# Issuing the first products of two blocks together in the even steps of chunk 0 of a pooled-attention and squared-ReLU kernel

## The chip, the cores and the metric

The kernel runs on one core of one Trainium2 chip. The metric is device time in microseconds (us) of one execution; less is better. The times shown are those of three runs of the same kernel, and one more execution was taken with the hardware profiler; the rows below come from that one.

## The reference

Inputs are q, k and v (8 batches, 8 heads, 576 tokens, 64 channels per head) and two weight matrices, `w_in` (512 x 2048) and `w_out` (2048 x 512), in float32.

```python
k_p = k.reshape(B, H, Sp, pool, D).mean(axis=3)        # pool = 8, Sp = 72
v_p = v.reshape(B, H, Sp, pool, D).mean(axis=3)
scores = scale * np.matmul(q, k_p.transpose(0, 1, 3, 2))
attn = np.exp(scores - np.max(scores, axis=-1, keepdims=True))
attn = attn / (np.sum(attn, axis=-1, keepdims=True) + 1e-09)
x = np.matmul(attn, v_p)          # heads side by side: 4608 tokens x 512
h = np.maximum(x @ w_in, 0.0)     # "first product"
out = h * h @ w_out               # "second product"
```

## The kernel before, in words

The 4608 tokens are worked on in 12 chunks of 384 tokens (`CH`, `NCH`). For each chunk the attention part makes x, kept transposed (channels on partitions, tokens along the free axis). The feed-forward part then goes through the 2048 hidden channels in 16 blocks of 128 (`NFC`). One pair (chunk, block) is a **step**; steps are numbered s = 16 x chunk + block, so steps 0 to 15 are chunk 0.

In a step, `hidden` (line 502) issues the first product of block s on TensorE (PE) into a PSUM bank, tile `h`, from the pool `ps_h`, which has two banks (line 100). From block 6 of chunk 0 on (`SPLIT = 6`) each float32 operand is split into a high and a low part (tiles `xh`, `xl` and `w_i`), and the first product is 12 matmuls: 4 pieces of 128 channels, three products each. The first six of the 12 read the weight tile `w_i_0`, the other six `w_i_2`; blocks 6 and 7 read the same two tiles, as do 8 and 9, and so on. `project` (line 539) issues the second product of block s - 2 (`LAG = 2`) into the output banks `o`. In chunk 0 it is 3 plain float32 products (6 rows in the trace), which read the block's activations `r` and the weight tile `wf_o`.

The function that `hidden` returns, `activate`, is called at the end of the step: ScalarE (ACT) reads the bank `h`, writes its ReLU to `r`, and squares it. Only that read of `h` makes the bank free for the block after the next.

Between `hidden` and `project` stand the PE parts of the attention for later chunks, which `on_pe` names: turning q (`qps`), scores (`sps`), turning the exponents (`pps`, `token_turn`) and weighing the values (`av`). Their PSUM tiles share three banks (`ps_a`). After the PE rows of a step come its rows on the other engines, in the order of the loop at the end of the program: reading those banks, the softmax, and the preparation of weights. In chunk 0 the weights still come in as 64-bit words, and each is turned to float32 and split: `magnitude` on ACT, `to_float32` on VectorE (DVE), and a cast on ACT with a subtraction on DVE in `split_weights`. The weights for chunk 0 are made just ahead of the blocks that read them, so in these steps ACT and DVE are as loaded as PE.

Every engine works through its own rows in program order (`InOrder`, line 23). The attention of chunk 1 has, for each pair of heads p, five stages in five steps from step 3p on: turn q; scores (`token_scores`) with the row maxima `tm` on DVE and the exponents `te` on ACT; `token_normalise` on DVE; `token_turn`; `weigh_values`. Pair 3's scores lie in step 10, its normalising in step 11, its turn in step 12 and its values in step 13. From step 10 the attention of chunk 2 begins: q of pair 0 is turned in step 10 and split into `st` (ACT, then DVE), and read by the scores in step 11; q of pair 1 in step 14, scores in step 15.

Of the kernel before, what the change touches and what calls it, by code (L numbers as in the profile page):

```python
# [37 lines left out]
def pooled_attn_relu2_ffn(  # L38
# [25 lines left out]
    NFC = DFF // P  # L64
# [19 lines left out]
    SPLIT = 6  # L84
# [37 lines left out]
    def issue_loads():  # L122
        for dst, src in loads:
            dma(dst, src)
        loads.clear()
# [39 lines left out]
    def to_float32(*keys):  # L165
        parts = []
        for key in keys:
            words, m = raw.pop(key).rearrange("p a (n w) -> p a n w", w=2), wf[key].rearrange("p (a n) -> p a n", a=2)
            parts.append((words, m, m.bitcast(U32)))
        for _, m, _ in parts:  # L170
            DVE.tensor_scalar(m, m, EXP_MIN, EXP_MAX, op0=ALU.max, op1=ALU.min)
        for words, _, m in parts:
            DVE.scalar_tensor_tensor(m, m, 3, words[..., 0], op0=ALU.logical_shift_left, op1=ALU.bitwise_or)
        for words, _, m in parts:
            DVE.scalar_tensor_tensor(m, words[..., 1], 0x80000000, m, op0=ALU.bitwise_and, op1=ALU.bitwise_or)
# [326 lines left out]
    def hidden(c, fc):  # L502
        hp = ps_h.tile([P, 512], F32, name=f"h_{c}_{fc}", tag="h")
        cb, o = fc * P // WC, fc * P % WC
        prods = []
        for cc in range(NCC):
            key, cols = ("i", cb, cc // 2 * 2), slice(cc % 2 * WC + o, cc % 2 * WC + o + P)
            if c == 0 and fc < SPLIT:
                prods += [(wf[key][:, cols], x0[cc // 2][:, cc % 2, :])]
            else:  # L510
                prods += [(wt[key][:, w, cols], xts[c][x][:, cc, :]) for w, x in ((0, 0), (0, 1), (1, 0))]
        for i, (w, x) in enumerate(prods):
            PE.matmul(hp[:, :CH], lhsT=w, rhs=x, start=i == 0, stop=i == len(prods) - 1)

        def activate():
            if c == 0:
                r = sb.tile([P, CH], F32, name=f"r_{c}_{fc}", tag="gh", bufs=LAG + 1)
            else:
                r = sb.tile([P, CH], F32, name=f"r_{c}_{fc}", tag="r", bufs=2)
            ACT.activation(r, hp[:, :CH], AF.Relu)  # L520
            if c < 2:
                ACT.activation(r, r, AF.Square)
            else:
                DVE.tensor_tensor(r, r, r, op=ALU.mult)
            gts[c, fc] = r

        return activate

    def split_hidden(c, fc):
        if c == 0:  # L530
            return
        gh = sb.tile([P, CH], F32R, name=f"gh_{c}_{fc}", tag="gh", bufs=LAG + 1)
        gl = sb.tile([P, CH], F32R, name=f"gl_{c}_{fc}", tag="gl", bufs=LAG + 1)
        split(gh, gl, gts[c, fc])
        gts[c, fc] = (gh, gl)
# [3 lines left out]
    def project(c, fc):  # L539
        if fc == 0:  # L540
            accs[c] = [ps_o.tile([P, 512], F32, name=f"o_{c}_{t}", tag=f"o{t}") for t in range(NTT)]
        g, key = gts.pop((c, fc)), ("o", fc)
        for t in range(NTT):
            tt = slice(t * P, (t + 1) * P)
            if c == 0:
                prods = [(g[:, tt], wf[key])]
            else:
                prods = [(g[x][:, tt], wt[key][:, w, :]) for x, w in ((0, 0), (0, 1), (1, 0))]
            for i, (a, w) in enumerate(prods):
                PE.matmul(accs[c][t], lhsT=a, rhs=w, start=fc == 0 and i == 0, stop=fc == NFC - 1 and i == len(prods) - 1)  # L550

        def store():
            for t in range(NTT):
                ob = sb.tile([P, DM], F32, name=f"ob_{c}_{t}", tag="ob", bufs=OB)
                ACT.copy(ob, accs[c][t])
                dma(out[c * CH + t * P:c * CH + (t + 1) * P, :], ob)

        return store if fc == NFC - 1 else None


    steps = [(c, fc) for c in range(NCH) for fc in range(NFC)]
# [105 lines left out]
    for c in range(1, NCH):  # L667
# [6 lines left out]
        for p in range(NPAIR):  # L674
            s = c * NFC + first[p]
# [5 lines left out]

    last = (to_float32, split_weights)
    on_pe = (transpose_k, transpose_q, scores, token_scores, token_turn, weigh_values)
    for s in range(-PRO, len(steps) + LAG):
        todo = work.get(s, [])
        activate = hidden(*steps[s]) if 0 <= s < len(steps) else None
        later = [f(*a) for f, a in sorted(((f, a) for f, a in todo if f in on_pe), key=lambda x: x[0] is weigh_values)]
        store = project(*steps[s - LAG]) if s >= LAG else None
        if 0 <= s - 1 < len(steps):
            split_hidden(*steps[s - 1])  # L690
        for f in later:
            f()
        for f, a in todo:
            if f not in on_pe + last:
                f(*a)
        keys = [a[0] for f, a in todo if f is to_float32]
        if keys:
            to_float32(*keys)
        for f, a in todo:
            if f is split_weights:  # L700
                f(*a)
        issue_loads()
        for f in (activate, store):
            if f:
                f()
# [30 lines left out]
```

## Time and profile before

| | us |
|---|---|
| median of 3 runs | 964.59 |
| lowest and highest | 963.69, 967.23 |
| profiled execution, its own time | 964.33 |
| span in the profile of that execution | 962.6 |

| engine | busy us | share of the span |
|---|---|---|
| PE (matmuls) | 946.1 | 98% |
| DVE | 615.0 | 64% |
| ACT | 451.5 | 47% |
| GpSimd (POOL) | 348.8 | 36% |

Busy shares are means over the whole span. The stretch that the change touches, blocks 6 to 15 of chunk 0, lies between 74.2 and 133.2 us from the start of the span; there PE is busy 56.69 of 59.00 us, DVE 49.79 and ACT 47.48, at a granted PE clock of 1.00. PE's bars overlap, as a matmul is still draining when the next one enters, so that times on PE are best read from start to start.

### The profile page before, as it was taken

How to read it: one execution, taken by the hardware profiler on the slowest of the kernel's cores; microseconds unless marked ns; L12 is line 12 of the kernel's file. 1: busy time of each engine (PE TensorE's matmuls, PEld its weight loads, DVE VectorE, ACT ScalarE, POOL GpSimd, SP SyncE). 2: the span in 40 equal slices, each digit the busy share in tenths (PEclk: the TensorE clock that was granted, in tenths of full speed). 3: DMA queues.
4: the chain of work that ended last, by engine and by line, in shares of the span. 5: the costliest groups of instructions: out<-in, count | busy, mean ns of one | idle time of the engine just before them, and what ended most of it. 6: DMA issues, size and time to landing. Idle time of an engine off the chain costs nothing.

```text
span 962.6 us, 13481 instructions
## 1 busy us (share of the span) xinstructions
PE 946.1 (98%) x4944; PEld 803.6 (83%) x4944; DVE 615.0 (64%) x1028; ACT 451.5 (47%) x909; POOL 348.8 (36%) x215
## 2 busy tenths in 40 slices
PE   7899999999999999999999999999999999999998
PEld 6456668888888888888888888888888888888997
DVE  7889886667865566677765656767776565453221
ACT  3789776754444344444344344434443434532322
POOL 3800144444444434344353444344443534440000
PEclk9799999999999999999999999999999999999999
DMA  9963112113112112112112112112211110100000
GB/s 256 319 237 116 61 33 78 35 50 98 52 31 77 32 34 67 48 52 82 52 44 77 30 35 79 38 30 69 82 50 39 68 32 18 58 10 9 33 1 34
DMA packets 51651, 63.65 MB, mean 66 GB/s; under 512 B 13936, under 2 KB 32192, under 8 KB 51584
## 3 DMA queue, kind: packets, MB, share of 16 engines
q1 hardware_dynamic: 51584, 62.78, 21.2%
q8 instruction: 39, 0.64, 0.3%
q14 instruction: 28, 0.23, 0.1%
HBM read 53.08 MB, written 9.68 MB: 65 GB/s over the span
## 4 chain that ended last, share of the span: by engine, by line
PE 88%; DVE 5%; DMA 4%; ACT 2%; issue 1%; SPq 0%; ACTq 0%; DVEq 0%
PE o L34 41%; PE h L34 39%; PE av L34 3%; PE sps L34 3%; DVE wf_o L34 2%; DVE wf_i L34 1%; PE qps L34 1%; DMA raw_o<-in_moe_w_out_dram 1%; DMA v<-in_v_dram 1%; DMA k<-in_k_dram 1%; ACT te L34 1%; DMA vv<-in_v_dram 1%; DMA raw_i<-in_moe_w_in_dram 1%; DVE tm L34 1%; DVE w_i L34 1%
## 5 line engine op out<-in xcount | busy, mean ns | idle before, releaser
L34 PE MATMUL h<-xh,w_i 128*128 128x384 f32 x1488 | 416.9, 341 | 0.0
L34 PE MATMUL o<-w_o,gh 128*128 128x512 f32 x1056 | 334.8, 398 | 0.0
L34 PEld LDWEIGHTS h<-xh,w_i 128*128 128x128 f32 x1488 | 272.8, 188 | 10.6 <-issue 1.4
L34 POOL PARTITION_ALL_REDUCE tot<-sc x80 | 201.4, 2564 | 210.1 <-issue 199.6
L34 PE MATMUL h<-xl,w_i 128*128 128x384 f32 x744 | 249.9, 336 | 0.0
L34 PEld LDWEIGHTS o<-w_o,gh 128*128 128x128 f32 x1056 | 192.4, 188 | 51.9 <-issue 16.5
L34 POOL PARTITION_ALL_REDUCE mx<-sc x80 | 117.8, 1519 | 287.1 <-ACT sc L34 287.1
L34 DVE TENSOR_TENSOR gl<-r,gh 128x384 fp32r<-128x384 f32 x176 | 143.5, 815 | 109.1 <-ACT gh L34 108.9
L34 PE MATMUL o<-w_o,gl 128*128 128x512 f32 x528 | 209.1, 396 | 0.0
L34 DVE TENSOR_TENSOR r<-r 128x384 f32<-128x384 f32 x160 | 105.6, 660 | 109.1 <-ACT r L34 108.8
L34 ACT CAST gh<-r 128x384 fp32r<-128x384 f32 x176 | 90.4, 514 | 150.3 <-DVE r L34 149.8
L34 PEld LDWEIGHTS h<-xl,w_i 128*128 128x128 f32 x744 | 139.7, 188 | 10.6 <-issue 2.9
L34 ACT ACTIVATE r<-h 128x384 f32<-128x384 f32 x192 | 94.2, 491 | 100.5 <-PE h L34 99.1
L34 PEld LDWEIGHTS o<-w_o,gl 128*128 128x128 f32 x528 | 99.1, 188 | 22.1
L34 DVE TENSOR_TENSOR st<-qps,st 64x384 fp32r<-64x384 f32 x80 | 60.8, 760 | 59.1 <-ACT st L34 58.3
L34 ACT CAST st<-qps 64x384 fp32r<-64x384 f32 x80 | 59.5, 744 | 56.9 <-PE qps L34 56.5
L34 ACT CAST xh<-rb 128x384 fp32r<-128x384 f32 x40 | 20.5, 513 | 94.6 <-DVE rb L34 94.6
L34 ACT ACTIVATE sc<-sc 72x384 f32<-72x384 f32 x80 | 39.7, 525 | 46.4 <-DVE sc L34 46.4
L34 DVE TENSOR_REDUCE vp<-v 72x64 f32<-72x512 f32 x48 | 51.0, 1062 | 0.0
L34 PE MATMUL av<-sc,vp 72*64 72x384 f32 (+1 forms) x256 | 45.6, 436 | 3.6 <-ACT sc L34 2.1
L34 PE MATMUL o<-wf_o,r 128*128 128x512 f32 x96 | 44.4, 598 | 0.0
L34 DVE TENSOR_REDUCE kp<-k 96x64 f32<-96x512 f32 x42 | 43.8, 1043 | 0.2 <-DMA k<-in_k_dram 0.2
(82 smaller groups left out, 702.1 us busy)
## 6 DMA issues: line engine op xcount, KB each, us to landing
k<-in_k_dram SPq DMA_DIRECT2D x48, 192.0 KB
out_dram<-ob SPq DMA_DIRECT2D x36, 256.0 KB
raw_i<-in_moe_w_in_dram SPq DMA_DIRECT2D x16, 512.0 KB
raw_o<-in_moe_w_out_dram SPq DMA_DIRECT2D x16, 512.0 KB
v<-in_v_dram SPq DMA_DIRECT2D x56, 144.0 KB
rb<-rd SPq DMA_DIRECT2D x80, 96.0 KB
q<-in_q_dram SPq DMA_DIRECT2D x30, 192.0 KB
q<-in_q_dram SPq DMA_DIRECT2D x32, 96.0 KB
```

Source lines behind the costliest of these rows:

```text
L34: return lambda *a, **k: self.tc.keep_in_program_order(f(*a, **k))
```

## The change

For s from 6 to 14 in the even steps, `hidden` is called for block s and at once for block s + 1, and in the odd step that follows it isn't called. `activate` of each block stays where it was, at the end of the block's own step.

```diff
     on_pe = (transpose_k, transpose_q, scores, token_scores, token_turn, weigh_values)
+    ahead = {}
     for s in range(-PRO, len(steps) + LAG):
         todo = work.get(s, [])
-        activate = hidden(*steps[s]) if 0 <= s < len(steps) else None
+
+        two = SPLIT <= s < NFC and s % 2 == 0
+        for n in range(s, s + 1 + two):
+            if 0 <= n < len(steps) and n not in ahead:
+                ahead[n] = hidden(*steps[n])
+        activate = ahead.get(s)
```

The order of the rows on DVE, ACT, POOL and SP is the same before and after; only PE's rows move. In the rows below a name ends in a serial number, `h_7` is block 7 of chunk 0, `r_4` the activations of block 4, and `sps_3` pair 3's scores; the first row of each group of like rows stands for the group.

PE in steps 6 and 7, before:

```order
L34 MATMUL pps_1_0_825<-ident,te_1_738 72x96 x4
L34 MATMUL qps_2_835<-ident,q_2_644 128x96 x4
L34 MATMUL o_0_625<-wf_o_633,r_4_771 128x512
L34 MATMUL h_7_871<-xh_685,w_i_0_704 128x384
L34 MATMUL sps_2_0_884<-kf_185,st_2_846 96x72
L34 MATMUL av_1_894<-sc_1_843,vp_184 64x192 x2
L34 MATMUL o_0_625<-wf_o_633,r_5_809 128x512
```

The same place with the change:

```order
L34 MATMUL h_7_825<-xh_685,w_i_0_704 128x384
L34 MATMUL pps_1_0_838<-ident,te_1_738 72x96 x4
L34 MATMUL qps_2_848<-ident,q_2_644 128x96 x4
L34 MATMUL o_0_625<-wf_o_633,r_4_771 128x512
L34 MATMUL sps_2_0_884<-kf_185,st_2_859 96x72
L34 MATMUL av_1_894<-sc_1_856,vp_184 64x192 x2
L34 MATMUL o_0_625<-wf_o_633,r_5_809 128x512
```

Block 7's first product has gone ahead of `pps`, `qps` and the second product of block 4, straight behind block 6's. Steps 8, 12 and 14 are alike.

PE in steps 10 and 11, before:

```order
L34 MATMUL sps_3_0_1047<-kf_185,st_2_846 96x72
L34 MATMUL qps_0_1057<-ident,q_0_855 128x96 x4
L34 MATMUL av_2_1062<-sc_2_1009,vp_184 64x192 x2
L34 MATMUL o_0_625<-wf_o_850,r_8_975 128x512
L34 MATMUL h_11_1111<-xh_685,w_i_0_930 128x384
L34 MATMUL sps_0_0_1124<-st_0_1084,kl_322 72x384
L34 MATMUL o_0_625<-wf_o_850,r_9_1031 128x512
```

The same place with the change:

```order
L34 MATMUL h_11_1047<-xh_685,w_i_0_930 128x384
L34 MATMUL sps_3_0_1060<-kf_185,st_2_859 96x72
L34 MATMUL qps_0_1070<-ident,q_0_868 128x96 x4
L34 MATMUL av_2_1075<-sc_2_1009,vp_184 64x192 x2
L34 MATMUL o_0_625<-wf_o_863,r_8_988 128x512
L34 MATMUL sps_0_0_1124<-st_0_1097,kl_322 72x384
L34 MATMUL o_0_625<-wf_o_863,r_9_1031 128x512
```

Pair 3's scores and the turn of chunk 2's q now stand behind block 11's first product; between that turn (`qps_0`) and the scores that read its result (`sps_0`) there is now no first product.

## Rows read from the trace of the kernel before

**Rows 1.** The page, busy time by engine over the span.

```profile
PE 946.1 (98%) x4944; PEld 803.6 (83%) x4944; DVE 615.0 (64%) x1028; ACT 451.5 (47%) x909; POOL 348.8 (36%) x215
```

**Rows 2.** Waits of PE from 60 us to the end: us, times, longest.

```profile
PE av L34 <- ACT te L34: 1.6, 1, 1.6
PE pps L34 <- DVE te L34: 0.8, 1, 0.8
```

**Rows 3.** Chain that ended last, 60 to 170 us: start, us, what.

```profile
115.11 2.60 PE o L34 x6
117.71 2.09 PE h L34 x12
```

**Rows 4.** Timeline of PE, steps 6 to 8: start, us, row, count.

```profile
76.73 0.82 PE L34 MATMUL pps<-ident,te 96*72 96x96 f32 x8
...
86.41 0.74 PE L34 MATMUL h<-xh,w_i 128*128 128x384 f32 x1
...
88.92 2.74 PE L34 MATMUL o<-wf_o,r 128*128 128x512 f32 x6
```

**Rows 5.** Timeline of ACT, steps 6 to 12; in brackets idle before, and releaser.

```profile
76.56 0.48 ACT L34 ACTIVATE r<-h 128x384 f32<-128x384 f32 x1
...
84.48 1.78 ACT L34 ACTIVATE te<-sps,tm 96x72 f32<-96x72 f32 x8 [1.97 <-DVE tm L34]
...
89.26 0.52 ACT L34 ACTIVATE r<-h 128x384 f32<-128x384 f32 x1
...
98.36 0.54 ACT L34 ACTIVATE r<-h 128x384 f32<-128x384 f32 x1
...
111.68 0.49 ACT L34 ACTIVATE r<-h 128x384 f32<-128x384 f32 x1
```

**Rows 6.** Timeline of PE, steps 2 and 3.

```profile
49.73 2.85 PE L34 MATMUL h<-x,wf_i 128*128 128x384 f32 x8 [1.17 <-ACT r L34]
...
56.20 2.85 PE L34 MATMUL h<-x,wf_i 128*128 128x384 f32 x8 [1.04 <-ACT r L34]
```

**Rows 7.** Timeline of PE, steps 10 to 12.

```profile
99.36 0.90 PE L34 MATMUL sps<-kf,st 64*96 64x72 f32 x16
...
102.29 0.87 PE L34 MATMUL av<-sc,vp 72*64 72x192 f32 x8 [1.56 <-ACT te L34]
...
107.86 0.34 PE L34 MATMUL sps<-st,kl 128*72 128x384 f32 x1
...
110.73 0.74 PE L34 MATMUL h<-xh,w_i 128*128 128x384 f32 x1
...
112.01 0.51 PE L34 MATMUL h<-xh,w_i 128*128 128x384 f32 x2
...
114.14 0.96 PE L34 MATMUL pps<-ident,te 96*72 96x96 f32 x8 [0.76 <-DVE te L34]
```

**Rows 8.** Timeline of DVE, steps 10 and 11.

```profile
100.55 0.46 DVE L34 TENSOR_REDUCE tm<-sps 96x4 f32<-96x288 f32 x1
...
104.68 1.77 DVE L34 TENSOR_TENSOR st<-qps,st 64x384 fp32r<-64x384 f32 x2 [2.91 <-ACT st L34]
...
111.04 1.31 DVE L34 TENSOR_TENSOR w_i<-wf_i,w_i 128x512 fp32r<-128x512 f32 x1
...
113.54 0.82 DVE L34 TENSOR_TENSOR te<-te,tm 96x288 f32<-96x288 f32 x2
```

**Rows 9.** Timeline of PE, steps 14 and 15.

```profile
125.30 0.50 PE L34 MATMUL qps<-ident,q 96*128 96x96 f32 x4
...
130.32 0.34 PE L34 MATMUL sps<-st,kl 128*72 128x384 f32 x1
```

**Rows 10.** Timeline of DVE, step 14.

```profile
127.56 1.72 DVE L34 TENSOR_TENSOR st<-qps,st 64x384 fp32r<-64x384 f32 x2 [1.76 <-ACT st L34]
```

**Rows 11.** Windows of PE: length, busy us (rows), granted clock, DMA share, GB/s.

```profile
30.00:35.00 5.00, 3.38 (x13) 0.79 1.02 333
35.00:40.00 5.00, 4.65 (x17) 0.50 1.04 394
40.00:45.00 5.00, 5.00 (x19) 0.69 1.07 350
45.00:50.00 5.00, 3.83 (x27) 1.00 0.85 262
```

## The prediction

> **What bounds the kernel now.** I read the page first: PE is busy for 98% of the span [rows 1], so the time ends where PE's rows end, and a change of order pays only by the idle time of PE that it removes or adds. The waits of PE come next. From 60 us to the end there are two, 1.6 us for the exponents `te` on ACT and 0.8 us for the normalised `te` on DVE [rows 2]; both lie in the stretch that the change touches. So the most that this change can give back is 2.3 us of 964, or 0.24%. Then the lengths on PE, from the chain of waits: a second product of chunk 0 takes 2.60 us and a first product 2.09 us [rows 3]. Below, H7 is the first product of block 7, P4 the second product of block 4. The timelines of ACT and DVE come last: each `activate` row stands far behind the first product that it reads. H8 begins at 86.41 us [rows 4], while the ReLU of block 7, the block before it, runs from 89.26 to 89.78 us [rows 5]. ACT and DVE lag behind PE by most of a step here, and PE works on because the order before gives it other work in between.
>
> **What the change does.** It adds and removes no instruction, on any engine; DVE, ACT, POOL and SP (with every DMA) keep their order. On PE, H7, H9, H11, H13 and H15 each move ahead of the attention rows and the second product of the even step. That does two things. The moved H needs its PSUM bank one second product and the step's attention rows earlier. And in an even step everything behind the moved H, attention rows and P, comes 2.09 us later, so that whoever reads those attention rows gets them later. The rows of an odd step come at the old time, unless PE was held.
>
> **Costs, one by one,** as lateness of PE against its old times.
>
> *H7.* It now follows H6 directly, where `pps` stood, at 76.73 us [rows 4]. Its bank is free when the ReLU of block 5 ends, at 76.56 + 0.48 = 77.04 us [rows 5]. That PE does wait for such a ReLU is seen in steps 2 and 3, by 1.17 and 1.04 us [rows 6]. Wait: 77.08 - 76.73 = **0.35**. Queued behind it are `pps`, `qps` and P4; ACT gets `pps` 2.09 + 0.35 = 2.44 late.
>
> *H9.* H8 ended at 88.92, where P6 starts [rows 4], so H9 stands ready at 88.92 + 0.35 = 89.27. It needs the ReLU of block 7, which ended at 89.78 [rows 5]. ACT has become 2.44 late in step 6, but had a pause of 1.97 ahead of the exponents at 84.48 [rows 5]; 0.47 is left and the ReLU ends at 90.25. Wait: **1.0**. If ACT absorbs all, it is 0.5; if nothing, 2.95. I take 1.0, since the pause is in the trace. PE is 1.35 late.
>
> *H11, H13, H15* find their bank free. For H11: the ReLU of block 9 ended at 98.90 [rows 5], with 1.35 more 100.25; H11 stands ready where `sps` stood, 99.36 + 1.35 = 100.71 [rows 7]. For H13: the ReLU of block 11 ended at 112.17 [rows 5], with the 3.15 of step 10 below 115.32; H13 comes after 116. A rule of the Trainium skill (Perfetto Trace Analysis, Optimization Strategy) speaks against the change here: it says that a gap which repeats regularly on the engine that should be saturated can mean too few buffers for the next tile. With two banks, five pairs and 0.35 to 1.0 a pair, that would make 1.75 to 5 us; by the rows only two pairs pay, together 1.35, and I go by the rows.
>
> *Step 10, the exponents.* Pair 3's scores start at 99.36 + 1.35 + 2.09 = 102.80 and last 0.90 [rows 7], to 103.70. Before, DVE came to them at 100.55, just 0.3 after they were done [rows 8]: it was DVE that was late. Now DVE waits for PE and is 103.70 - 100.55 = 3.15 late, and with it all that hangs on it. `av`, which waits for a bank that the exponents free, comes at 102.29 + 3.15 = 105.44; so the old wait of 1.56 [rows 7] is hardly shortened.
>
> *Step 11, scores of chunk 2.* They need `st`, which DVE ended at 104.68 + 1.77 = 106.45 [rows 8], now 109.60. H11 covered that before; now only P8 does (105.44 + 0.87 + 2.60 = 108.91). They start at 109.60 and not at 107.86 [rows 7]: PE is 1.74 late.
>
> *H12.* It starts at 110.73 + 1.74 = 112.47 [rows 7]. Its 7th matmul, 1.45 later (112.01 - 110.73 to the 6th [rows 7], and 2.09 / 12 = 0.17 more), reads the second weight tile, which DVE ended at 111.04 + 1.31 = 112.35 [rows 8], just in time; now 115.50. Wait: 115.50 - 113.92 = **1.6**, lateness 3.3. This is the least certain term. DVE's row of 1.31 ran beside a reduction on POOL, which comes later too: from 0 to 1.6, and I take all of it.
>
> *Step 12, the normalised exponents.* They are ready at 113.54 + 0.82 + 3.15 = 117.51 [rows 8]; `pps` now comes at 115.50 + 1.04 + 2.09 = 118.63, so the old wait of 0.76 [rows 7] is gone. Against 114.14 + 2.09, PE is 2.4 late.
>
> *Steps 14 and 15.* `qps` starts at 125.30 + 2.4 + 2.09 = 129.79 [rows 9]. From its start to the end of DVE's `st` took 127.56 + 1.72 - 125.30 = 3.98 [rows 9, 10], and DVE was waiting for ACT, which had just got `qps` [rows 10], so the length stays. The scores can start at 133.77; PE has at most 0.50 + 2.60 to put in between, as H15 has gone ahead. Before, they started at 130.32 [rows 9]. Lateness **3.45**, 1.05 of it new.
>
> Beyond that PE has no wait to give back [rows 2], so it is not regained. **Sum:** 0.35 + 1.0 + 0.4 (step 11) + 1.6 - 0.9 (step 12) + 1.05 = about 3.45 us. Pairing two first products saves nothing itself: 2.09 + 2.60 a step are already matmul after matmul. The profiled execution took 964.33 us, so 964.33 + 3.45 = **967.8 us**; the median of the runs is 0.26 above the profiled time, within their spread. That is 0.35% more, and about 0.5% (4.8 us) is what a measurement here can tell from no change.
>
> **Rivals.**
>
> *The waits only change place* (963 to 965.5). DVE and ACT take up the lateness as they do after step 7, H12 finds its weights, and PE loses 1.35 at the banks and 1.05 in step 15, and wins back up to 2.3 [rows 2]: 964.4. For it: DVE had 2.91 of waiting in step 10 [rows 8]. Against: that waiting hangs on the exponents themselves, which come later.
>
> *Slower by over 0.5%, through ACT* (969.7). The lateness of step 6 isn't absorbed: the cast that DVE needs ahead of pair 2's maxima sits behind the late `pps` rows on ACT, so the pause at 84.48 moves along instead of shrinking [rows 5]. H9 then waits 2.95 instead of 1.0 and all behind it is 1.95 later: 967.8 + 1.95. It decides once the ReLU of block 7 ends after about 91.9 us.
>
> *Slower through the clock* (972.9). From 35 to 40 us PE had a granted clock of 0.50, the 1.2 GHz level, after 3.38 busy of 5 us; the shortfall over 30 to 45 us is 5 x (0.21 + 0.50 + 0.31) = 5.1 us [rows 11]. If the new waits bring that on, 967.8 + 5.1. The Trainium skill (TensorE: Matmul & The Clock Gate, Why this matters for your kernels) warns that idle gaps between bursts of matmuls bring the slow clock back. Against it: waits of 1.17 and 1.04 us [rows 6] passed at a clock of 1.00 in 45 to 50 us [rows 11], and the new ones are mostly of that size, five in 60 us.
>
> *Faster by over 0.5%* would need 4.8 us, and PE has only 2.3 us of waits to lose.
>
> **How the numbers follow.** Forecast 0.63, waits that change place 0.17, ACT 0.11, clock 0.06, something unseen that is faster 0.03. The forecast and the second case lie within 0.5% (0.80); the two slower rivals lie outside (0.17). The range runs from 964.4, the second case's value, to 971.5: the upper bound of the H9 term with 1.8 for a part of a clock loss or a second such wait. It leaves out most of the clock case and the lower half of the second.
>
> **What would show it.** Right: waits of PE for the ReLU at H7 and H9; `tm` of pair 3 starting right after `sps` near 103.7; a wait of `h` for `w_i` at H12; a wait of `sps` for `st` of about 1 us in step 15; no `pps` wait in step 12; clock 1.00. Wrong: no wait at H9, DVE back on its old times by 115 us, PE at block 0 of chunk 1 before 134.5 (it was at 133.2; I expect 136.6), or a clock below 1 there.

## The result and the profile after

| | before | changed |
|---|---|---|
| median of 10 runs, us | 964.86 | 968.10 |
| lowest and highest, us | 963.49, 970.45 | 967.80, 969.27 |
| ratio of the times, 95% interval | | 1.0034 (1.0021 to 1.0047) |
| profiled execution, span, us | 962.6 | 966.1 |
| start of H6, the first product of block 6 | 74.22 | 73.54 |
| start of block 0 of chunk 1 | 133.20 | 136.20 |
| the stretch between the two | 58.98 | 62.66 |

The forecast was 967.8 us, with 3.45 us more in the stretch. The stretch has 3.68 more in the two profiles, and the medians differ by 3.24. That is less than the 0.5% that the prediction took as the least to be told from no change, but the whole interval of the ratio lies above 1, so the changed kernel is slower. The rows that bound the stretch, in the kernel before and then in the changed one:

```profile
74.22 0.74 PE L34 MATMUL h<-xh,w_i 128*128 128x384 f32 x1
...
133.20 0.74 PE L34 MATMUL h<-xh,w_i 128*128 128x384 f32 x1
```

```profile
73.54 0.74 PE L34 MATMUL h<-xh,w_i 128*128 128x384 f32 x1
...
136.20 0.74 PE L34 MATMUL h<-xh,w_i 128*128 128x384 f32 x1
```

Behind the stretch the two profiles hardly differ: 962.6 - 133.20 = 829.4 us and 966.1 - 136.20 = 829.9 us.

As H6 itself starts at a slightly different time in every execution (0.68 us earlier in that of the changed kernel), places are compared below by their distance from H6.

First the waits of PE from 60 us to the end, in the changed kernel (engine, line, releaser: us, times, longest):

```profile
PE av L34 <- ACT te L34: 1.3, 1, 1.3
PE h L34 <- ACT r L34: 1.3, 2, 1.1
PE sps L34 <- ACT w_i L34: 1.0, 1, 1.0
```

Beside [rows 2]: the wait for the exponents `te` has stayed, that of `pps` for the normalised exponents has gone, and two kinds are new, first products that wait for a ReLU, and the scores of step 15. The releaser that the last line names is a cast on ACT that had nothing to do with them; the split of q on DVE is what ended just before, as its row below shows.

PE's timeline in the changed kernel (start, us, row; in brackets idle before and releaser):

```profile
76.39 0.44 PE L34 MATMUL h<-xh,w_i 128*128 128x384 f32 x1 [0.18 <-ACT r L34]
...
78.60 0.82 PE L34 MATMUL pps<-ident,te 96*72 96x96 f32 x8
...
89.93 0.44 PE L34 MATMUL h<-xh,w_i 128*128 128x384 f32 x1 [1.08 <-ACT r L34]
...
92.14 2.74 PE L34 MATMUL o<-wf_o,r 128*128 128x512 f32 x6
...
102.57 0.90 PE L34 MATMUL sps<-kf,st 64*96 64x72 f32 x16
...
105.25 0.87 PE L34 MATMUL av<-sc,vp 72*64 72x192 f32 x8 [1.30 <-ACT te L34]
106.05 4.54 PE L34 MATMUL o<-wf_o,r 128*128 128x512 f32 x6
109.80 0.96 PE L34 MATMUL sps<-st,kl 128*72 128x384 f32 x1
...
115.28 0.61 PE L34 MATMUL h<-xh,w_i 128*128 128x384 f32 x2
...
118.19 0.82 PE L34 MATMUL pps<-ident,te 96*72 96x96 f32 x8
...
133.30 0.37 PE L34 MATMUL sps<-st,kl 128*72 128x384 f32 x1 [1.01 <-ACT w_i L34]
```

These answer to [rows 4, 7, 9]. H7 and H9 wait where the prediction put them (in step 8 there are no attention rows, so H9 passes P6 alone). The row at 106.05 is new in another way: P8's bar is 4.54 us long, where that of P6, the same six rows, has 2.74 in [rows 4].

ACT's timeline, to be read beside [rows 5]:

```profile
75.86 0.48 ACT L34 ACTIVATE r<-h 128x384 f32<-128x384 f32 x1
...
79.13 0.92 ACT L34 COPY sc<-pps 72x384 f32<-72x384 f32 x2 [2.23 <-PE pps L34]
...
84.61 1.77 ACT L34 ACTIVATE te<-sps,tm 96x72 f32<-96x72 f32 x8 [0.43 <-DVE tm L34]
...
89.39 0.49 ACT L34 ACTIVATE r<-h 128x384 f32<-128x384 f32 x1
```

ACT now waits 2.23 us for `pps`, as H7 stands ahead of it, and the old pause of 1.97 us ahead of the exponents has shrunk to 0.43.

DVE's timeline, beside [rows 8, 10]:

```profile
83.25 0.69 DVE L34 TENSOR_TENSOR w_i<-wf_i,w_i 128x512 fp32r<-128x512 f32 x1 [0.73 <-ACT w_i L34]
...
103.50 0.45 DVE L34 TENSOR_REDUCE tm<-sps 96x4 f32<-96x288 f32 x1 [2.48 <-PE sps L34]
...
107.63 1.70 DVE L34 TENSOR_TENSOR st<-qps,st 64x384 fp32r<-64x384 f32 x2 [2.91 <-ACT st L34]
...
113.92 1.31 DVE L34 TENSOR_TENSOR w_i<-wf_i,w_i 128x512 fp32r<-128x512 f32 x1
...
131.45 1.71 DVE L34 TENSOR_TENSOR st<-qps,st 64x384 fp32r<-64x384 f32 x2 [3.82 <-ACT st L34]
```

The maxima of pair 3 now wait 2.48 us for PE, where DVE came to them late before, and the rows behind them follow at their old distances. In the last row `st` ends at 133.16, and the scores of step 15 start at 133.30.

And the granted clock of PE (length, busy, clock, DMA share, GB/s):

```profile
106.00:107.00 1.00, 1.00 (x4) 0.92 0.03 8
107.00:108.00 1.00, 1.00 (x2) 0.50 0.00 0
108.00:109.00 1.00, 1.00 (x3) 0.50 0.00 0
109.00:110.00 1.00, 1.00 (x4) 0.50 0.00 0
110.00:111.00 1.00, 1.00 (x5) 0.87 0.00 0
```

For some 3.4 us PE ran at half speed, the 1.2 GHz level, just behind the wait for the exponents. Summed over these windows that is 0.08 + 3 x 0.50 + 0.13 = 1.7 us of PE's work lost. The prediction had this as a rival that adds 5.1 us to the rest. Did these 1.7 us make the time, in place of the waits that I had predicted?

### The profile page after: what moved, and what is told of

It reads as the page before. It is cut to its first block, busy times and chain, and to the rows that moved or that the text cites. A ratio compares the mean times of both kernels' runs of the same rounds, so it can differ in the third digit from the quotient of the medians.

```text
span 966.1 us, 13480 instructions
## 1 busy us (share of the span) xinstructions
PE 947.9 (98%) x4944; PEld 803.5 (83%) x4944; DVE 614.4 (64%) x1028; ACT 451.4 (47%) x909; POOL 348.9 (36%) x215
## 4 chain that ended last, share of the span: by engine, by line
PE 88%; ACT 4%; DMA 3%; DVE 3%; SPq 1%; issue 1%; DVEq 0%; ACTq 0%
PE o L34 40%; PE h L34 39%; PE av L34 3%; PE sps L34 3%; DMA raw_i<-in_moe_w_in_dram 2%; PE qps L34 1%; DVE wf_o L34 1%; DMA k<-in_k_dram 1%; SPq L34 1%; ACT te L34 1%; DVE wf_i L34 1%; DMA q<-in_q_dram 1%; ACT r L34 0%; ACT wf_o L34 0%; ACT st L34 0%
```

## The experiments

Theory A is the prediction's: the moved first product waits for its bank, and the attention rows behind it reach DVE late, whose chain then sets when block 12 gets its weights. Theory B: the fall of the clock is the cost. Theory C: pairing costs a fixed amount per pair. D and E are named where they are tested. Each kernel was timed beside the kernel before on the same chip, whose median there was 964.15 to 964.44 us; the ratio is that of the two times. "Stretch" is from H6 to block 0 of chunk 1 in the one execution that was profiled, where before has 58.98 us.

### The gap filled, so that the clock holds (fill_wait)

```diff
         qt = loaded.pop(("q", c, p))
+        for i in range(8 if (c, p) == (2, 0) else 0):
+            PE.matmul(pt[:, :P], lhsT=ident, rhs=ident, start=True, stop=True)
```

> The changed kernel with 8 matmuls of the identity put on PE in step 10 ahead of the turn of chunk 2's q, into the bank that the turn then overwrites; 1.1 us of PE work where PE waited 1.3 us for the exponents. Theory A: the clock stays at 1.00 from 106 to 111 us, and the time stays as in the changed kernel (968.1 us, within 0.5), because the second weight tile of block 12 is ready at 115.2 us either way: the freed 1.7 us turns up as a wait of H12 of about 1.5 us. Theory B: the time falls by about 1.7 us to 966.4 us.

Measured: 967.77 us, ratio 1.0043 (1.0028 to 1.0058), stretch 62.77 (H6 at 74.08, block 0 at 136.85). Its windows (as above, with PE, PEld, DVE, ACT and POOL busy ahead of the clock) and its waits:

```profile
104.00:108.00 4.00, 4.00 (x32) 3.12 (x31) 1.14 (x4) 3.19 (x10) 0.00 (x0) 1.00 0.00 2
108.00:112.00 4.00, 3.78 (x12) 1.80 (x11) 3.77 (x7) 3.94 (x10) 0.00 (x0) 1.00 0.00 0
```

```profile
PE h L34 <- ACT r L34: 1.3, 2, 1.1
PE sps L34 <- ACT w_i L34: 1.0, 1, 1.0
PE h L34 <- DVE w_i L34: 0.9, 1, 0.9
PE sps L34 <- DVE st L34: 0.4, 2, 0.2
```

Rows of PE, then the row of DVE that H12 waits for:

```profile
103.95 2.05 PE L34 MATMUL qps<-ident 128*128 128x128 f32 x16
...
106.26 0.87 PE L34 MATMUL av<-sc,vp 72*64 72x192 f32 x8
```

```profile
115.21 0.68 DVE L34 TENSOR_TENSOR w_i<-wf_i,w_i 128x512 fp32r<-128x512 f32 x1
```

The clock stayed at 1.00, and the time didn't move. The 1.7 us came out again in three places. The eight matmuls took 1.89 us (the turn of q follows at 105.84) and not the 1.1 expected, so that `av` starts 0.47 us later than in the changed kernel, by the distance from H6 (106.26 - 74.08 against 105.25 - 73.54). The scores of step 11 wait for `st` (0.2 in the list), and H12 waits for `w_i` (0.9). These two are waits that the prediction had and that the changed kernel's list doesn't show: slow PE filled them there. What ends both kernels' delay is the same tile: DVE's `w_i` ends 41.69 us after H6 in the changed kernel and 41.81 here. Theory B, 966.4 us, falls for the changed kernel.

### The waits for the banks taken away (relu_early)

```diff
         for f in later:
             f()
+        if s in (5, 7):
+            activate()
+            activate = None
         for f, a in todo:
```

> The changed kernel, but in steps 5 and 7 the activation (ReLU and square) stands on ScalarE right behind the attention rows of the step, ahead of the work on the weights. Only ScalarE's order in two steps differs. Theory A: the waits ahead of H7 and H9 (0.2 and 1.1 us) are gone, all that follows on PE, VectorE and ScalarE comes 1.2 to 1.3 us earlier, and the stretch from H6 to block 0 of chunk 1 falls from 62.66 to 61.4 us; 966.8 us. Theory D (what binds from step 10 on is VectorE's own load, and an earlier PE doesn't help): unchanged, 968.1 us.

Measured: 966.11 us, ratio 1.0026 (1.0003 to 1.0049), stretch 60.79 (73.72 to 134.51). Its waits:

```profile
PE av L34 <- ACT te L34: 1.3, 1, 1.3
PE sps L34 <- ACT w_i L34: 1.0, 1, 1.0
PE sps L34 <- DVE st L34: 0.2, 1, 0.2
```

The two waits are gone, and the stretch is 1.87 shorter, more than the 1.26 that the idle column of the changed kernel had shown for them (0.18 + 1.08). By the starts it is 0.50 at H7 (H6 to `pps`: 5.06 us in the changed kernel, 4.56 here) and 1.37 at H9 (H8 to P6, 92.14 - 86.20 = 5.94 and 90.45 - 85.88 = 4.57), together 1.87: all of it reached block 0 of chunk 1. The idle column counts from the end of the last bar, while without a wait the next row starts before that end, and so it leaves out about 0.3 us of each such wait. The interval of the ratio is too wide to tell A from D; the trace does: DVE's `w_i` for block 12 ends 39.83 us after H6 (112.24 + 1.31 - 73.72), 1.86 earlier than in the changed kernel, so an earlier PE does help and theory D falls.

### The second first product behind the attention rows (behind_attention)

```diff
-        for n in range(s, s + 1 + two):
-            if 0 <= n < len(steps) and n not in ahead:
-                ahead[n] = hidden(*steps[n])
+        if 0 <= s < len(steps) and s not in ahead:
+            ahead[s] = hidden(*steps[s])
...
+        rows = [(f, a) for f, a in todo if f in on_pe]
+        later = [f(*a) for f, a in rows if f is not weigh_values]
+        if two:
+            ahead[s + 1] = hidden(*steps[s + 1])
+        later += [f(*a) for f, a in rows if f is weigh_values]
```

> All five pairs, but in an even step the second first product stands behind the attention rows that VectorE and ScalarE wait for (pps, qps, sps) and ahead of the values and the second product. Theory A: no wait at H7, 1.1 us at H9 as step 8 has no attention rows, none for the exponents in step 10 as H11 covers it, none for the split q in step 15, so of the 3.7 us that the stretch from H6 to block 0 of chunk 1 has gained about 1.0 is left (the H9 wait, and VectorE's own path to the weights of block 12 and the normalised exponents of step 12, which is 0.8 late): 60.0 us against 58.98 before and 62.66 changed; 965.3 us. Theory C (the cost lies in pairing itself): 62.7 us and 968.1.

Measured: 965.63 us, ratio 1.0008 (0.9993 to 1.0023), stretch 61.25 (73.76 to 135.01).

```profile
PE h L34 <- DVE w_i L34: 1.0, 1, 1.0
PE pps L34 <- DVE te L34: 0.8, 1, 0.8
PE h L34 <- ACT r L34: 0.8, 1, 0.8
```

All five second first products still stand in the even step (only H9 directly behind its H8), and most of the cost is gone: the interval leaves out theory C's 968.1. The waits at H7, for the exponents and in step 15 are gone; that at H9 is left, and so are the two in step 12 that DVE's chain sets, as expected. Up to `pps` of step 12 the lateness is 0.79 (114.47 - 73.76 against 114.14 - 74.22), near the 1.0 expected; 1.48 more came behind it, where H13 took 3.23 us from start to start at a lower clock (windows as above):

```profile
114.00:115.00 1.00, 0.53 (x4) 0.76 0.00 0
115.00:116.00 1.00, 1.00 (x7) 0.50 0.00 0
116.00:117.00 1.00, 1.00 (x4) 0.50 0.00 0
117.00:118.00 1.00, 1.00 (x5) 0.53 0.00 0
```

Here a slow clock did cost in the profiled execution: no wait of PE comes behind it in the stretch that could hide it.

### One pair at a time (pairs_6_8, pair_10, pair_12, pair_14)

The only edit is the condition:

```diff
-        two = SPLIT <= s < NFC and s % 2 == 0
+        two = s in (6, 8)
```

and `s == 10`, `s == 12`, `s == 14` in the others.

> Only blocks 6+7 and 8+9 are paired. Theory A (the bank of the moved first product is not yet read by ScalarE, and the attention rows behind it reach VectorE late): PE waits for a ReLU ahead of H7 by 0.2 us and ahead of H9 by 1.1 us, block 0 of chunk 1 starts about 1.0 to 1.3 us later than the 133.2 us of before, 965.3 us. Theory B (the low clock after a gap of PE is the cost): no low clock without the pair of step 10, so no more than 0.3 us, 964.7 us. Theory C (each pair costs the same, a fifth of 3.4 us): 1.4 us, 965.8 us.

> Only blocks 10+11 are paired. Theory A: pair 3's maxima start on VectorE near 102.4 instead of 100.55 us, the second weight tile of block 12 is ready 1.9 us later, H12 waits for it, and the old wait of step 12 stays as there is no moved H13: block 0 of chunk 1 1.9 to 2.1 us late, 966.3 us. Theory B: 1.7 us if the clock falls to 0.5 behind the wait of the values, nothing if it doesn't. Theory C: 0.7 us, 965.0 us.

> Only blocks 12+13 are paired. Theory A: H13 covers the wait for the normalised exponents (0.8 us by the wait, 0.9 by the starts) and nothing else changes: the stretch falls from 58.98 to 58.1 us, 963.4 us. Theory C (each pair costs the same): 0.7 us more, 965.0 us.

> Only blocks 14+15 are paired. Theory A: the scores of chunk 2 in step 15 wait 1.05 us for the split q, as the length from the turn to the end of the split is 3.98 us and PE has only 2.9 us of work in between; 965.4 us. Theory B: nothing, 964.4 us. Theory C: 0.7 us, 965.0 us.

> The same kernel as in the run of the pair 14+15 alone, with more rounds, since there the median (968.4) and the stretch from H6 to block 0 of chunk 1 (60.54 us) did not agree. Theory A: the stretch is 60.0 to 60.6 us and the median about 1.2 to 1.6 us over the kernel before, 965.7 us; the 968.4 came from a start that was slow in those executions (H6 at 77.1 us). Theory E (pairing the last two blocks costs something behind the stretch too): again over 967.5 us, with H6 near 74 us and the rest after block 0 of chunk 1 longer than the 829.4 us of before by 2 us.

| kernel | stretch, us | difference from before | median, us | ratio (95%) |
|---|---|---|---|---|
| pairs_6_8 | 61.15 | +2.17 | 965.82 | 1.0017 (0.9992 to 1.0041) |
| pair_10 | 60.73 | +1.75 | 965.88 | 1.0028 (1.0010 to 1.0047) |
| pair_12 | 59.64 | +0.66 | 963.75 | 0.9997 (0.9983 to 1.0011) |
| pair_14 | 60.54 | +1.56 | 968.40 | 1.0046 (1.0030 to 1.0062) |
| pair_14_again | 60.50 | +1.52 | 966.41 | 1.0022 (1.0007 to 1.0037) |

The waits are where theory A has them: 0.22 and 1.05 us for the ReLU at H7 and H9 in pairs_6_8, none new in pair_10 but that the maxima come late, by 1.81 us (102.27 - 74.13 against 100.55 - 74.22), the wait of `pps` gone in pair_12, and in pair_14 the one at the scores of step 15:

```profile
PE av L34 <- ACT te L34: 1.3, 1, 1.3
PE sps L34 <- DVE st L34: 1.2, 2, 1.0
```

Pair_10's stretch has about this lateness, 1.75, near the 1.9 to 2.1 expected. But the sizes came out too large for pairs_6_8, pair_12 and pair_14 by 0.5 to 1.6 us, and the four differences sum to 6.1, not to the 3.68 of all pairs together. In each of these profiles the clock had fallen behind the wait of step 10, also in pair_12 and pair_14, where nothing differs from the kernel before up to there:

```profile
104.00:108.00 4.00, 4.00 (x8) 0.60 0.00 0
```

(pair_12: 1.6 us of work lost, which is the distance between the 58.1 expected and the 59.64 measured.) So pairs_6_8, pair_12 and pair_14 tell the places of the waits, not their sizes, and their times alone don't tell A from C. A profile is one execution, too: that of pair_12 took 965.14 us where the median was 963.75, and the one profile of the kernel before, with no fall of the clock here, may not stand for all its executions. How often the clock falls was not measured. Of the two runs of pair_14 the first had four timed executions only; the profile of the second, with H6 as late as 79.99 us, has nearly the same stretch, and the rest of its span, 970.4 - 140.49 = 829.9 us, is near that of before (829.4). So E falls, and what made the first median high lies ahead of H6 (at 77.14 us in that profile), where the kernels don't differ.

### The kernel before with the gap filled (before_fill)

The edit of fill_wait, on the kernel before.

> The kernel before with the 8 filling matmuls of the identity in step 10 ahead of the turn of chunk 2's q. Theory A: where the clock falls behind the wait of step 10 it costs the kernel before less than it takes (1.7 us less the 0.9 us wait of step 12 that it hides, 0.8 us); with the fill the clock is 1.00 from 102 to 110 us in the profile and the time is the kernel before's or up to 0.8 us less. Theory B: 1.7 us less, 962.6 us.

Measured: 963.72 us beside 964.28, ratio 0.9990 (0.9975 to 1.0006); stretch 58.49 (76.78 to 135.27), clock 1.00 from 100 to 112 us, no wait of PE left in the list from 60 us on. The median is 0.56 us less and the stretch 0.49. The interval, from 2.4 us less to 0.6 more, holds no change, theory A's up to 0.8 and theory B's 1.7 alike, so the times don't decide here. The profile of the kernel before had the clock at 1.00 in step 10 without a fill, so the two stretches don't price a fall either.

### First products moved only to where PE waited (covered, covered_pe)

```diff
-        later = [f(*a) for f, a in sorted(((f, a) for f, a in todo if f in on_pe), key=lambda x: x[0] is weigh_values)]
+        rows = sorted(((f, a) for f, a in todo if f in on_pe), key=lambda x: x[0] is weigh_values)
+        later = [f(*a) for f, a in rows if f is not weigh_values]
+        if s == 10:
+            ahead[11] = hidden(*steps[11])
+        later += [f(*a) for f, a in rows if f is weigh_values]
...
-        for f in later:
-            f()
+        keys = [a[0] for f, a in todo if f is to_float32]
+        for n, f in enumerate(later):
+            f()
+            if s == 10 and rows[n][0] is token_scores:
+                to_float32(*keys)
+                keys = []
...
-        keys = [a[0] for f, a in todo if f is to_float32]
```

with `two = s == 12`. The call of `to_float32` behind the scores, which changes DVE's order, is left out in covered_pe.

> A version meant to beat both: first products are moved ahead only where PE waited. H11 stands behind the scores of pair 3 and the turn of q and ahead of the values (step 10), H13 ahead of the turn of the exponents (step 12), all else as before; and on VectorE the step 10 work that makes float32 weights stands right behind the maxima, where VectorE waited 2.9 us, ahead of the split of q. Theory A: both old waits (1.6 and 0.8 us) go, none comes, the stretch falls from 58.98 to 56.9 us; 962.2 us. If the split q gets late by VectorE's moved work, 0.5 of that is lost. Theory D: the stretch stays at 58.9 us.

> The version with H11 behind the scores and the turn of q and H13 ahead of the turn of the exponents, with VectorE's order left as before. Theory A: the waits for the exponents and the normalised exponents go, but VectorE has the second weight tile of block 12 ready only at its old time, so H12 waits 1.2 us; the stretch is 57.9 us, between the 58.98 of before and the 56.83 of the version with VectorE's order changed too; 963.2 us. If the order on VectorE does nothing, 56.9 us and 962.1.

Measured: covered 962.08 us, ratio 0.9970 (0.9955 to 0.9985), stretch 56.83 (74.58 to 131.41); covered_pe 963.00 us, 0.9983 (0.9970 to 0.9997), stretch 57.93 (73.60 to 131.53). The waits of PE in covered, then in covered_pe:

```profile
PE sps L34 <- DVE st L34: 0.3, 1, 0.3
```

```profile
PE h L34 <- DVE w_i L34: 1.0, 1, 1.0
PE sps L34 <- DVE st L34: 0.2, 1, 0.2
```

Covered beats both kernels: 0.30% under before, and by the medians, taken at different times, 6 us under the changed kernel. With PE's order alone H12 waits for DVE's weights; moving DVE's own rows into its pause of 2.9 us [rows 8] brings the last 1.1 us of the stretch (the intervals of the two ratios overlap). In both, H13 stands right behind H12 as in the change, and it costs nothing there: against theory C.

## Why the prediction was right

The number (967.8 against 968.10), the sign and the range held, and so did the mechanism: relu_early, pair_10 and behind_attention take its delays away or show one alone, and the time follows. That the sum came so near is in part luck, as the terms at H7 and H9 were too small and that of H12 too large. Of the signs named beforehand, the waits at H7 and H9, the maxima right behind `sps`, the wait in step 15 and the missing `pps` wait came; a wait of `h` for `w_i` at H12 and a clock of 1.00 did not. By its steps, as lateness of PE or DVE against the old distance from H6 (2.09 us taken off where a moved first product stands in between, as in the prediction):

| place | predicted | measured | rows of the changed kernel |
|---|---|---|---|
| H7, seen at `pps` | 0.35 | 0.46 | 78.60 |
| H9, seen at P6 | 1.35 | 1.81 | 92.14 |
| maxima of pair 3 on DVE | 3.15 | 3.63 | 103.50 |
| scores of step 11 | 1.74 | 2.62 | 109.80 |
| `pps` of step 12 | 2.4 | 2.64 | 118.19 |
| scores of step 15 | 3.45 | 3.66 | 133.30 |
| block 0 of chunk 1 | 3.45 | 3.68 | 136.20 |

*H7 and H9: right in kind, under-sized.* Part of the H9 term was how much of ACT's lateness the pause at 84.48 takes up. I took 1.97 of it; 0.43 of the pause was left over, unused. The exponents wait for DVE's maxima, and DVE had itself waited 0.73 us for ACT's late cast: the way that the ACT rival described, at a small price. The exponents came 0.81 us late (84.61 + 0.68 against 84.48), where I had 0.47. The ReLU of block 7 ended at 89.39 + 0.49 = 89.88 us, or 90.56 on the clock of the kernel before, where I had 90.25 and the ACT rival needed 91.9.

*The maxima: right.* They start 0.03 us after `sps` ends (102.57 + 0.90, then 103.50), so DVE now waits for PE.

*Steps 11 and 12: the sum near, the terms not as told.* From P6 to `pps` of step 12 I had 2.4 - 1.35 = 1.05 more, and 0.83 came. In it I had 0.39 for the scores of step 11 and 1.6 for H12; neither shows as a wait in the changed kernel's list. The clock fell instead, and P8 and the first row of the scores took about 1.7 us longer (4.55 us from 106.05 to 110.60; in the kernel before, P8 and the first row behind it, H11's, take 2.86). The fill shows that this is the same time spent another way: with the clock held, waits of 0.2 and 0.9 come up and the stretch stays at 62.77. DVE's second weight tile ends at 113.92 + 1.31 = 115.23 and PE goes on at 115.28; how early PE gets there is of no account. The term of H12 was also over-sized by two matmuls: DVE makes the low half of the weights, which isn't read by the 7th matmul but by the 9th, 0.35 us later, as the place of the 115.28 row in H12 shows.

*The clock rival was wrong in its arithmetic.* The fall, which I had thought unlikely, did come, behind step 10 in the changed kernel and in six more of the profiles above, and behind step 12 in behind_attention; the 972.9 us did not. The loss was 1.7 us and not 5.1, and I added its whole price to the forecast, though the forecast itself already held PE back at the same place for another reason. Two delays of PE ahead of one late tile don't add up. That the price is real where no such tile is late shows in behind_attention (1.48 us in one profile). What I held against the fall was also read too early: the windows of [rows 11] end at 50 us, 0.3 us behind the wait of 1.17 and ahead of that of 1.04. The next two, given at the end, do show a clock of 1.00.

*"Waits only change place"* fell: pair_10 and the trace show that DVE couldn't take the lateness up. *No gain from pairing itself* held: covered and covered_pe, the only runs clearly faster than before, gain by moving first products into waits.

A rule of the Trainium skill was weighed in the prediction (Perfetto Trace Analysis, Optimization Strategy: gaps that repeat can mean too few buffers). The trace agrees in two pairs of five, with waits for a bank of 0.50 and 1.37 us by the starts. In relu_early even these went without a further bank, by reading the bank earlier in ACT's order.

## What to carry to other kernels

Moving work ahead on the bound engine delays all that it passes; look up who on the other engines waits for the passed rows and whether those had slack (here 0.3 us at the maxima of pair 3, and 1.0 at the split q of step 15, against 2.09 of delay). Move a piece into a wait, behind the rows that others need and ahead of the row that waits: H11 and H13, moved in this way, then gave 1.4 us, and 2.2 with the other engine's rows put into its own pause. And a loss in front of a late result is no extra cost: to price two delays, ask first whether they end at the same event.

## What the runs showed of the hardware that I had not expected

Behind a wait of PE of 1.3 to 1.6 us in step 10, with only small matmuls (`sps`, `qps`, `av`) around it, the clock fell to the 1.2 GHz level for some 3 us in seven of the eight profiles that have this wait; the kernel before, whose profile shows the wait of 1.56 us at a clock of 1.00, is the eighth. In the five profiles in which PE had work there (fill_wait, before_fill, behind_attention, covered, covered_pe) it stayed at 1.00 from 100 to 108 us. In behind_attention it fell later, behind two waits of 0.95 and 0.78 us in step 12. The Trainium skill (TensorE: Matmul & The Clock Gate, Why this matters for your kernels) names idle gaps between bursts as what brings the slow clock; the trace agrees in kind.

Not every such wait did it. The kernel before waited 1.17 us between small `sps` rows and a first product, and 1.04 us between a second product and a first one [rows 6], and the windows behind show 1.00:

```profile
50.00:55.00 5.00, 5.00 (x14) 1.00 1.05 375
55.00:60.00 5.00, 3.96 (x22) 1.00 1.02 386
```

What beside the gap decides was not tried.
